# Half-row mask matmuls, casts with heads outermost and a new order of the first quarter in an attention and gated MLP kernel

## The chip, the cores and the metric

The kernel runs on one core of one Trainium2 chip. The metric is device time in microseconds, the median of several runs. A core has five engines that run side by side, each in its own order: TensorE (PE; its weight loads are shown as PEld), VectorE (DVE), ScalarE (ACT), GpSimd (POOL) and SyncE (SP, which here only issues DMAs). Profiles use the short names.

## The reference

Four sequences of 768 tokens with 8 heads of 64: causal attention, in which heads 0, 2 and 6 see everything before them and the other five see only the first 4 tokens and the last 64. Its output, 3072 rows of 512, goes through a two-layer MLP with the gate h / (1 + exp(-beta h)).

```python
scores = scale * np.matmul(q, k.transpose(0, 1, 3, 2))
rel = pos[:, None] - pos[None, :]
stream_keep = (rel >= 0) & ((pos[None, :] < 4) | (rel < 64))
scores = np.where(mask, scores, -1e9)      # mask: causal, or stream_keep
a = softmax(scores); x = a @ v             # then heads side by side: 3072 x 512
h = x @ w_in                               # 512 -> 2048
out = (h / (1 + np.exp(-beta * h))) @ w_out
```

## The kernel before

**Chunks and units.** The work is cut into 8 chunks (a half of a sequence, 384 rows, in three tiles of 128), taken in an order in which two sequences alternate. A chunk has 4 units of two heads each. Unit u belongs to chunk u // 4; units 0 to 7 (chunks 0 and 1) are the first halves of the first two sequences, so all their keys lie in their own 384 rows. The two heads of a unit lie in partitions 0 to 63 and 64 to 127 of KT and QT, so the two score matmuls of a pair use different row halves of TensorE.

**One unit** goes through: a load of q and k in float32 (SP, four heads at a time, into a tile s0 or s1 with the layout k/q, head, tile, 64), a cast to bf16 into qkb (L246), three transposes on TensorE each for k and q (L322), copies out of PSUM to KT (L330) and QT (L333), scores into a pair of PSUM banks sp in two steps (L451), exponentials on ACT into es (L460), the products with the values (L532), a division (L541, L545) that gives x, and for two units at a time the transposes of x (L570) and their copy to xT (L579). Streaming heads also need the sink tokens' keys and values beside the window's (KO, L312; VO, L259 and L260).

**Masks.** In chunks 0 and 1 a mask is added ahead of the scores: a matmul with the identity as weights (L422; "sp<-Ns,idb", "sp<-Nc,idb") writes 0 or -1e9 into the bank, and the scores are accumulated on top. Nc is causal, Ns has the three kinds of block of a streaming head. Unit 5 is an exception: its mask is multiplied after the exponential (L478, the word "ma"). From unit 8 on all masks are multiplied (Mh, Mc).

**MLP.** With xT of a chunk, G1 makes 16 groups of 128 features: four matmuls of 384 columns (L600), tanh on ACT (L605), and the gate on DVE (L608). G2 (L653) sums over the 16 and ends in a scaled copy (L657) and a store (L659). The weights come in four quarters each, by DMAs that POOL issues (L140 w_in, L144 w_out); a quarter of w_in holds four groups. The first 32 groups run as eight of chunk 0, eight of chunk 1, the other eight of chunk 0, the other eight of chunk 1.

**Order.** The order on every engine is the order in which the program emits instructions; there is no other scheduler. The first quarter is written out by hand in the string RAMP, one word per step, and the rest in PLAN. A word is a kind, a unit or chunk, for some a part, and an engine (v, a, g): ck and cq cast k or q, tk and tq transpose, kk and kq copy out of PSUM, ko copies sink keys, ad opens a pair of score banks and adds the mask, qk the scores, ex the exponentials, ma multiplies masks, pv a third of the value products, no divides, xx and cx transpose and copy x, cv and vo cast and copy values, lq and lv load, wi and wo issue a quarter of the weights, ro a piece of chunk 2's or a later chunk's rows, mm, mA and mb run a group of G1 (into mm or into an sp bank) or a step of G2, hm and hf the halves of one group, be the transposes of beta, ne, on and ml prepare masks and ones, and zz issues matmuls of zeros that keep TensorE busy.

**Buffers.** qkb has four buffers, so unit u's cast waits for the transposes of unit u - 4. PSUM has two pairs of banks sp for scores and three single banks mm for everything else of the ramp. QT has three buffers.

## Time and profile before

| | |
|---|---|
| median of 3 runs | 229.45 us (228.44, 229.45, 230.8) |
| profiled execution: span, first to last instruction | 227.0 us; 2.45 us below the median of the runs; its device time is not listed by itself |
| TensorE clock granted | 0.999 of full |
| PE, PEld busy | 219.4 us (97%), 126.4 us (56%) |
| DVE, ACT, POOL busy | 142.1 us (63%), 154.0 us (68%), 87.3 us (38%) |
| chain that ended last | PE 89%, DMA 4%, DVE 2%, SP's queue 2% |
| DMA | 31.66 MB, mean 139 GB/s |

Busy time of PE adds up what instructions take from start to end, and matmuls overlap in its pipeline, so the spacing of their starts tells what each really occupies. A line such as "14.50 0.51 PE L322 MATMUL mm<-idb,qkb 128*128 128x128 bf16 x6" in the order of time reads: start, length, engine, line, operation, output from inputs, size of the weights, the moving operand, and how many; what stands in brackets is idle time of that engine ahead of it and what ended it. The rows of a grouped view give busy time in us, the mean in ns, and idle time before.

### The profile page before, as it was taken

The numbers are of one execution on the slowest core, as the hardware profiler recorded it, in microseconds if no ns is written. First come the engines' busy times: TensorE is split into PE (matmuls) and PEld (weight loads), VectorE is DVE, ScalarE is ACT, GpSimd is POOL, SyncE is SP. The second block draws the span as 40 slices with busy tenths as digits, with TensorE's granted clock in tenths as the row PEclk, the third lists the DMA queues.
The fourth block names the chain that finished last, engine by engine and source line by source line (L and its number), as shares of the span: only waits on it lengthen the run. The fifth ranks groups of instructions, "written<-read, shape, count | busy, mean of one in ns | idle before, by whom it ended". The sixth has DMA issues, their size and how long they took to land.

```text
span 227.0 us, 5019 instructions
## 1 busy us (share of the span) xinstructions
PE 219.4 (97%) x1898; PEld 126.4 (56%) x1917; DVE 142.1 (63%) x342; ACT 154.0 (68%) x254; POOL 87.3 (38%) x143
## 2 busy tenths in 40 slices
...
GB/s 204 262 301 239 225 197 198 195 220 171 149 216 178 161 153 144 141 175 133 103 131 162 126 151 140 92 133 103 216 64 107 24 81 0 49 46 46 0 49 92
DMA packets 95383, 31.66 MB, mean 139 GB/s; under 512 B 81776, under 2 KB 92416, under 8 KB 95360
## 3 DMA queue, kind: packets, MB, share of 16 engines
...
q10 hardware_dynamic: 576, 0.40, 0.6%
...
## 4 chain that ended last, share of the span: by engine, by line
PE 89%; DMA 4%; DVE 2%; SPq 2%; issue 1%; ACT 0%; ACTq 0%; DVEq 0%
PE mm L653 34%; PE mm L600 25%; PE sp L600 12%; PE sp L451 6%; PE po L532 6%; DMA s<-in_k_dram 3%; DMA s<-in_q_dram 2%; PE mm L638 2%; DVE es L478 1%; PE mm L322 1%; SPq L132 1%; PE mm L570 1%; PE mm L451 1%; SPq L119 1%; PE sp L422 1%
## 5 line engine op out<-in xcount | busy, mean ns | idle before, releaser
L653 PE MATMUL mm<-w_out_sb,gT 128*128 128x512 bf16 x349 | 84.1, 379 | 1.3 <-issue 0.5
L460 ACT ACTIVATE es<-sp 128x768 bf16<-128x768 f32 (+2 forms) x72 | 56.5, 837 | 19.6 <-PE sp L451 19.4
L600 PE MATMUL mm<-xT,w_in_sb 128*128 128x384 bf16 x348 | 64.6, 326 | 0.0
L600 PEld LDWEIGHTS <-w_in_sb 128*128 128x128 bf16 x512 | 47.8, 98 | 29.7 <-issue 0.2
L605 ACT ACTIVATE th<-mm,beta_h 128x384 f32<-128x384 f32 x87 | 49.8, 588 | 5.6 <-PE mm L600 0.9
L653 PEld LDWEIGHTS <-gT 128*128 128x128 bf16 x368 | 33.4, 98 | 36.0 <-issue 1.5
L608 DVE SCALAR_TENSOR_TENSOR gT<-th,mm 128x384 bf16<-128x384 f32 x87 | 46.8, 551 | 7.4 <-ACT th L605 3.8
L282 POOL DMA_DIRECT2D s<-in_q_dram x30 | 22.4, 761 | 27.2 <-DMA QTD<-s 21.7
L600 PE MATMUL sp<-xT,w_in_sb 128*128 128x384 bf16 x164 | 32.3, 326 | 0.0
L657 ACT ACTIVATE osb<-mm 128x512 f32<-128x512 f32 x23 | 13.8, 602 | 26.1 <-PE mm L653 25.8
L532 PEld LDWEIGHTS <-es 128*128 128x128 bf16 x472 | 23.3, 98 | 13.6 <-issue 1.5
L608 DVE SCALAR_TENSOR_TENSOR gT<-th,sp 128x384 bf16<-128x384 f32 x41 | 22.3, 552 | 5.6 <-ACT th L605 3.7
L532 PE MATMUL po<-VX,es 128*128 128x65 bf16 x360 | 24.9, 194 | 0.8 <-ACT VX L251 0.4
L605 ACT ACTIVATE th<-sp,beta_h 128x384 f32<-128x384 f32 x41 | 23.8, 586 | 2.3 <-PE sp L600 0.2
L282 POOL DMA_DIRECT2D s<-in_k_dram x30 | 22.4, 759 | 6.8 <-DMA w_out_sb<-in_moe_w_out_dram 5.2
L251 POOL CAST VX<-vs 128x512 bf16<-128x512 f32 x16 | 10.6, 662 | 34.6 <-DMA vs<-in_v_dram 31.8
L541 DVE RECIPROCAL rec<-po 128x6 f32<-128x6 f32 x28 | 5.4, 193 | 27.0 <-PE po L532 27.0
L478 DVE TENSOR_TENSOR es<-es,Mh 128x768 bf16<-128x768 bf16 (+1 forms) x26 | 17.4, 698 | 5.0 <-ACT es L460 4.4
L451 PE MATMUL sp<-QTD,KT 64*128 64x128 bf16 (+2 forms) x258 | 19.2, 240 | 0.6 <-ACT QTD L333 0.3
L545 DVE TENSOR_TENSOR x<-po,rec 128x384 bf16<-128x384 f32 x28 | 15.6, 557 | 1.0
L451 PEld LDWEIGHTS <-KT 64*128 64x128 bf16 x278 | 11.1, 94 | 5.8 <-issue 3.6
L259 POOL COPY VO<-VX 128x512 bf16<-128x512 bf16 x16 | 10.0, 649 | 7.3 <-DVE VX L251 7.3
...
## 6 DMA issues: line engine op xcount, KB each, us to landing
...
```

Source lines behind the costliest of these rows:

```text
L251: copy(out=VX[b % 2][:, h2 * HT + t, :, 0:D], in_=staged["v", c][:, t])
L282: nc.gpsimd.dma_start(out=ROWS[c % 2, name][:, t, i * 4 * D:(i + 1) * 4 * D].rearrange("p (h d) -> p h d", d=D), in_=src[b, i:H:2, r:r + 1 ...
L451: nc.tensor.matmul(sps[i][r][:, x * 128:y * 128], key(a, lhs), s["QT"][half(a), qi * 128:(qi + y - x) * 128], start=first, stop=first or y ...
L460: nc.scalar.activation(out=views[i].rearrange("p r k j -> p r (k j)"), in_=banks[2][:, :, 0:n * 128], func=ACTF.Exp, scale=scale)
L478: nc.vector.tensor_mul(ev[:, :, 0:n], ev[:, :, 0:n], Mh[h2][:, None, m0:m0 + n].to_broadcast([128, 2, n, 128]))
L532: nc.tensor.matmul(po[:, qi, hh, :], e, val, start=(j == 0), stop=(j == len(lst) - 1))
L545: nc.vector.tensor_mul(xg[g][:, :, :, u % 2, :].rearrange("p a t d -> p t a d"), po[:, :, :, 0:D], rec.to_broadcast([128, HT, 2, D]))
L600: nc.tensor.matmul(hp[:, 0:HALF], w_in_sb[:, mo, fi * 128:(fi + 1) * 128], xT[c][:, mo, :], start=(mo == 0), stop=(mo == MO - 1))
L605: nc.scalar.activation(out=th, in_=hp[:, 0:HALF], func=ACTF.Tanh, scale=beta_h[:, fi:fi + 1])
L608: nc.vector.scalar_tensor_tensor(out=gTs[c][:, fi, :], in0=th, scalar=1.0, in1=hp[:, 0:HALF], op0=ALU.add, op1=ALU.mult)
L653: nc.tensor.matmul(op, gTs[c][:, fi, ns * 128:(ns + 1) * 128], w_out_sb[:, fi, :], start=(fi == 0), stop=(fi == FO - 1))
L657: nc.scalar.activation(out=osb, in_=op, func=ACTF.Copy, scale=0.5)
```

## The change

- **Masks of units 0 to 7.** Nq holds the kinds of block (causal, and three for streaming heads), made on POOL; folded() copies it into Nt, whose halves hold, for row half r and query half h, a block's weights for one head. An addition is now, per head and block, two matmuls with 64 rows of Nt as weights and 64 columns of the identity as moving operand (128 columns where one block serves two tiles). The two heads of a unit use the two row halves, in turns. Unit 5 is masked in this way too; "ma" is gone from the ramp. The masks Mh and Mc for later units are made later, on POOL (late_masks).
- **Casts.** qkb holds k first, and the cast walks heads outermost, so that it reads 192 consecutive numbers at a time. cast_both casts k and q of a unit in one instruction: units 0 (ACT), 1 and 3 (DVE) and 5 (POOL).
- **Order.** RAMP is new, with fillers as words (zi). PLAN is not touched. The matmuls of zeros read one block of 128 columns four times.

Two functions for two units at once (words wk, wq, yk, yq) and an engine for masks are added and not used by the new RAMP. The core of the diff:

```diff
...
         both = stage.tile([128, 2, 4, HT, D], F32, name=f"s{g}")
+        both_of[c, g] = both
...
+    zeros = consts.tile([128, 128], BF16, name="zeros")
+    nc.vector.memset(zeros, 0.0)
+    still = zeros[:, None, :].to_broadcast([128, 4, 128])
...
-    zeros = consts.tile([128, 512], BF16, name="zeros")
-    nc.vector.memset(zeros, 0.0)
...
     def idle(n, pool, name):
         for i in range(n):
             nothing = pool.tile([128, 512], F32, name=name)
-            nc.tensor.matmul(nothing, zeros[:, 0:128], zeros, start=True, stop=True)
-    idle(9, ps_m, "mm")
+            nc.tensor.matmul(nothing.rearrange("p (n j) -> p n j", n=4), zeros, still, start=True, stop=True)
...
-    own_masks, old_mask = Mh[0][:, 0:3:2], Mh[0][:, 1]
-    nc.vector.memset(Mh[0][:, 0:3], 1.0)
-    select(own_masks, 1, -1, window_i - 1, 2)
-    select(old_mask, 1, -1, -(128 - window_i + 1), 1)
-    nc.gpsimd.memset(Mh[0][0:n_sink_i, 0:2], 1.0)
-    select(own_masks, -1, 1, 0, 2)
-
-    Ns = consts.tile([128, 5 * 128], BF16, name="Ns")
-    Nc = consts.tile([128, 256], BF16, name="Nc")
     Mc = consts.tile([128, 128], BF16, name="Mc")
-    nc.gpsimd.memset(Nc, 0.0)
-    nc.gpsimd.affine_select(out=Nc.rearrange("p (r j) -> p r j", r=2), in_=Nc.rearrange("p (r j) -> p r j", r=2), compare_op=ALU.is_ge, fill=NEG, base=0, pattern=[[0, 2], [1, 128]], channel_multiplier=-1)
-
-    def negatives(which):
-        if 2 in which:
-            nc.vector.tensor_scalar(out=Mc, in0=Nc[:, 0:128], scalar1=0.0, scalar2=None, op0=ALU.is_ge)
-        a, n = which[0], len(which)
-        nc.vector.tensor_scalar(out=Ns[:, a * 128:(a + n) * 128], in0=Mh[0][:, a % 3 + a // 3:3].rearrange("p r j -> p (r j)"),
-                                scalar1=-1.0, scalar2=-NEG, op0=ALU.add, op1=ALU.mult)
+
+    def late_masks(part):
+        if part == 0:
+            nc.gpsimd.memset(Mh[0][:, 0:3], 1.0)
+            nc.gpsimd.memset(Mc, 1.0)
+        if part == 1:
+            select(Mh[0][:, 0:3:2], 1, -1, window_i - 1, 2)
+            select(Mh[0][:, 1], 1, -1, -(128 - window_i + 1), 1)
+            nc.gpsimd.memset(Mh[0][0:n_sink_i, 0:2], 1.0)
+        if part == 2:
+            select(Mh[0][:, 0:3:2], -1, 1, 0, 2)
+            select(Mc, -1, 1, 0, 1)
+
+
+    Nq = consts.tile([128, 4, 128], BF16, name="Nq")
+    Nt = consts.tile([128, 2, 4, 128], BF16, name="Nt")
+
+    def negative(buf, cm, step_, base, n):
+        nc.gpsimd.affine_select(out=buf, in_=buf, compare_op=ALU.is_ge, fill=NEG, base=base,
+                                pattern=[[0, n], [step_, 128]][2 - min(n, 2):], channel_multiplier=cm)
+    nc.gpsimd.memset(Nq, 0.0)
+    negative(Nq[:, 0], 1, -1, 0, 1)
+
+    def negatives(part):
+        if part == 0:
+            negative(Nq[:, 1:3], -1, 1, window_i - 1, 2)
+            negative(Nq[:, 3], -1, 1, -(128 - window_i + 1), 1)
+            nc.gpsimd.memset(Nq[:, 2:4, 0:n_sink_i], 0.0)
+            negative(Nq[:, 1:3], 1, -1, 0, 2)
+
+    def folded(some, copy):
+        for r in range(2):
+            for h in range(2):
+                copy(out=Nt[64 * r:64 * r + 64, h, some], in_=Nq[64 * h:64 * h + 64, some])
...
-        copy(out=s["qkb"][:, "qk".index(name)], in_=staged[name, c, p // 2][:, p % 2:4:2].rearrange("p h t d -> p t h d"))
+        copy(out=s["qkb"][:, "kq".index(name)].rearrange("p t h d -> p h t d"), in_=staged[name, c, p // 2][:, p % 2:4:2])
...
+    def cast_both(u, copy):
+        c, p = u // NPAIR, u % NPAIR
+        s = st_u.setdefault(u, {})
+        s["qkb"] = att.tile([128, 2, HT, 2, D], BF16, name="qkb", bufs=4)
+        copy(out=s["qkb"].rearrange("p i t h d -> p i h t d"), in_=both_of[c, p // 2][:, :, p % 2:4:2])
...
+            todo = []
             for r in range(2) if u < 8 and u not in on_vector else ():
                 n = len(dict.fromkeys((e[2], e[5]) for e in tiles[i][r] if added(e)))
                 m = tiles[i][r][0][5]
-                neg = Nc[:, 0:n * 128] if m is None else Ns[:, m * 128:(m + n) * 128]
-                nc.tensor.matmul(sps[i][r][:, 0:n * 128], ident, neg, start=True, stop=False)
+                kinds = [(0, 0, n)] if m is None else [((2, 3, 1, 3, 1)[m + x], x, 1) for x in range(n)]
+                todo.append([(r, h, *y) for y in kinds for h in range(2)])
                 covered[i, r] = n
+            opened_ = set()
+            while any(todo):
+                for some in todo:
+                    if some:
+                        r, h, kind, x, n = some.pop(0)
+                        rows_ = slice(64 * r, 64 * r + 64)
+                        nc.tensor.matmul(sps[i][r][:, x * 128:(x + n) * 128].rearrange("p (n j) -> p n j", n=n)[:, :, 64 * h:64 * h + 64], Nt[rows_, h, kind],
+                                         ident[rows_, None, 64 * r:64 * r + 64].to_broadcast([64, n, 64]), start=(r not in opened_), stop=False)
+                        opened_.add(r)
...
+            ends = {r: (r, x, y) for r, x, y, e in seq}
             for r, x, y, (a, lhs, qi, val, diag, m) in seq:
-                first = x >= covered.get((i, r), 0)
+                whole = (i, r) not in covered
                 nc.tensor.matmul(sps[i][r][:, x * 128:y * 128], key(a, lhs), s["QT"][half(a), qi * 128:(qi + y - x) * 128],
-                                 start=first, stop=first or y == covered[i, r])
+                                 start=whole, stop=whole or (r, x, y) == ends[r])
...
-        def mask(i):
+        def mask(i, eng=nc.vector):
             ev = views[i]
             ms = [[x for x, e in enumerate(tiles[i][r]) if e[5] is not None] for r in range(2)]
             if ms[0] and ms[0] == ms[1]:
                 n = len(ms[0])
                 m0 = tiles[i][0][0][5]
-                nc.vector.tensor_mul(ev[:, :, 0:n], ev[:, :, 0:n], Mh[h2][:, None, m0:m0 + n].to_broadcast([128, 2, n, 128]))
...
     def keep_busy(n):
 
         for i in range(n):
-            nc.tensor.matmul(sums_bank(0), zeros[:, 0:128], zeros, start=True, stop=True)
+            nc.tensor.matmul(sums_bank(0).rearrange("p (n j) -> p n j", n=4), zeros, still, start=True, stop=True)
...
+        elif what == "cb":
+            cast_both(n, copies[eng])
...
-            negatives([(0, 1, 2), (3, 4)][n])
+            negatives(n)
+        elif what == "fo":
+            folded([slice(0, 1), slice(1, 4)][n], copies[eng])
+        elif what == "mh":
+            late_masks(n)
...
-            late[n].pop(0)()
+            late[n].pop(0)(copies[eng or "v"])
         elif what == "tt":
             run(steps_T(n))
+        elif what == "zi":
+            idle(n, ps_m, "mm")
         elif what == "zz":
             keep_busy(n)
...
     RAMP = """
-        ck0g ne1 lv0.0 lv0.1 tk0 ck2a ne0 cq0v ck1a zz3 tq0 kq0a zz3 ad0.0 on0v lv0.2 kk0v cq1v tq1 qk0.0 tk2 ad0.1
-        kq1v tk1 kk1v lq1.0g be qk0.1 ex0.0 zz3 ad1.0 cv0.0g ko1 lq1.1 ex0.1 pv0 ck3v cq3g tk3 lv1.0g cq2a tq2 kk3v
-        lv1.1 cv0.1g ad1.1 qk1.1 kk2v ex1.1 tq3 ko2 qk1.0 wi0 vo0 cq4g lv1.2 cv0.2a lq2.0g ko3 pv0 kq2v pv0 ad2.0
-        qk2.0 lv2.0 ex1.0 pv1 kq3a pv1 ck4v ad2.1 qk2.1 lv2.1 pv1 ex2.0 ad3.0 tq4 no0 tk4 ex2.1 ck7g kk4a qk3.0 ad3.1
-        qk3.1 no1 pv2 ck6v ex3.0 cq5v ck5g pv2 tk6 xx0 ad4.0 cq6g pv3 kq4v ex3.1 pv2 ad4.1 cx0v ad5.0 qk4.1 pv3 lv2.2
-        no2 on1g tq5 pv3 qk4.0 kk6a ml0 tk5 cq7g kq5v ex4.1 kk5a ko5 ko6 ad5.1 tq6 wi1 qk5.0 ex4.0 tk7 tq7 ex5.0 no3
-        qk5.1 ex5.1 kq6v xx1 ad6.0 kk7v wi2 kq7v wi3 cx1a qk6.0 ml1 ad6.1 ex6.0 cv1.1g ko7 qk6.1 cv1.0v ex6.1 hm lq2.1
-        ma5.0 ma5.1 mm cv1.2g vo1 mm wo0 pv4 lv3.0g ad7.0 lv3.1 pv4 hf pv4 no4 qk7.0 ad7.1 pv5 pv5 ex7.0 lv3.2 qk7.1
-        pv5 no5 ml1 wo1 ex7.1 pv6 pv6 wo2 mm pv7 rq pv7 pv7 no7 wo3 pv6 no6 rk cq8g xx2 ro3 cx2a mA mA ck8g xx3 cx3a
-        mm mA mm mA mm mm mA mm mm mm mA mm ro3 mm mm mA mm mm mm ro3 mA mm ro3 mA mm ro3 mm mm ro3 mA mA mb mb tt8 mb
-        mb mb
+        zi8 lv0.0 cb0a ne0 fo1v zz3 cb1v tk0 tq0 on0v tq1 fo0g lv0.1 ck2v lv0.2 zz2 cb3v tk1 lq1.0 ad0.0 ad0.1 zz3
+        kk0a kq0a tk2 qk0.0 kk1a kq1v lq1.1 kk2v qk0.1 cq2g ex0.0 be zz3 ad1.1 ko1 zz1 cv0.1g tq2 tk3 ex0.1 wi0 ko2
+        lv1.0g cv0.0v kq2v ad1.0 cv0.2v lv1.1 lv1.2 qk1.0 qk1.1 kk3v ex1.0 ex1.1 tq3 ad2.0 ck4v kq3a qk2.0 lq2.0 pv0
+        lv2.0 vo0 pv0 pv1 ad2.1 ex2.0 pv0 pv1 qk2.1 lv2.1 ad3.0 pv1 no0 pv2 cq4g cb5g ko3 ex2.1 tq4 no1 qk3.0 ex3.0
+        tk4 kk4v kq4a tq5 ad3.1 qk3.1 xx0 ad4.1 ck6v qk4.1 kq5v cq6a cx0v pv2 tk6 ex3.1 ck7g pv2 mh0 no2 ad4.0 tk5
+        mh1 pv3 pv3 cq7g on1v kk6v qk4.0 mh2 mlg pv3 tq6 kk5v lv2.2 ex4.1 ko5 ko6 ad5.0 qk5.0 ex4.0 wi1 no3 tq7
+        lq2.1 kq6a ad5.1 ex5.0 qk5.1 wo0 xx1 wi2 tk7 cv1.1g cx1v ad6.1 ml1 ex5.1 cv1.0v kq7a qk6.1 ex6.1 ad6.0 kk7a
+        qk6.0 mm mm cv1.2v ko7 ex6.0 lv3.0 pv4 hm vo1 wi3 pv4 hf pv4 pv5 pv5 no4 ad7.1 qk7.1 ad7.0 qk7.0 pv5 no5 pv6
+        pv6 ex7.0 pv6 ex7.1 wo1 mm wo2 pv7 no6 pv7 xx2 pv7 cx2a ml1 no7 mA ck8g rq wo3 mA rk xx3 mm cx3v mA mm lv3.1
+        mm mm ro3 mA mm mA ro3 mm ro3 mA lv3.2 ro3 mm mA mm mA mm mA mm mm mA cq8g mm mA mm ro3 mm mm ro3 mA mA mb
+        mb tt8 mb mb mb
     """
     words = RAMP.split()
     on_vector = {int(w[2]) for w in words if w.startswith("ma")}
```

40 lines of the change are left out of this document (32 added, 8 removed).

## The prediction

> **What bounds the kernel now.** I read the windows first, then the chain that ended last, then each engine in order of time. The columns of a window are its length, TensorE's busy time (instructions), the granted clock, the DMA share and GB/s.
>
> ```profile
> core 0: 227.0 us, clock 0.999
> 4.96:22.00 17.04, 15.74 (x203) 1.00 1.20 272
> 22.00:46.04 24.04, 24.04 (x200) 1.00 1.21 204
> 46.04:227.00 180.96, 176.00 (x1494) 1.00 0.88 117
> ```
>
> From 22.00 to 46.04 us TensorE never rests, at full clock, and after that for under 5 us in 181. The first 22 us are different: there the chain runs through loads, and from about 17 us on it is TensorE's own work:
>
> ```profile
> 1.32 4.09 DMA s<-in_q_dram
> 9.35 5.93 DMA s<-in_k_dram
> 17.13 0.15 PE po L532 x5
> 17.28 0.22 PE sp L422 x2
> 18.00 0.17 PE mm L322 x3
> 23.86 0.32 PE sp L422 x2
> ```
>
> These rows (start, length, what, count) also give what a matmul really occupies, which the busy times of single instructions, being latencies, do not: 30 ns for 65 columns (0.15 / 5), 56 for 128 (0.17 / 3), 110 for 256 (0.22 / 2), 160 for 384 (0.32 / 2).
>
> The built order of the changed kernel differs from the old one on TensorE only in its first part: the last 3105 of its rows are the same, one for one, and SP's list of DMAs is the same throughout. So the time changes by what happens up to there. I compare up to the last mark that both ramps have, the second x transposes (xx3, at 28.80 us in a row below), behind which L600 runs densely. A microsecond before it is a microsecond at the end, as TensorE hardly rests afterwards.
>
> **Where the first part hangs.** On the loads of chunk 1:
>
> ```profile
> 13.94 0.50 POOL L246 CAST qkb<-s 128x384 bf16<-128x384 f32 x1 [0.22 <-DMA s<-in_q_dram]
> 14.50 0.51 PE L322 MATMUL mm<-idb,qkb 128*128 128x128 bf16 x6
> ```
>
> Unit 4's q lands, is cast by 14.44, and its transposes (tq4) start at 14.50. In the new order tq4 stands at the same place, behind the same cast on POOL and the same load. Ahead of it stand the same scores, masks and value products, and one third of pv2 more (two 65-column matmuls, 0.06 us). So the questions are whether the new order reaches tq4 late, and how long it needs from there.
>
> **Up to tq4: half a microsecond of cover.** Fillers and casts:
>
> ```profile
> 1.29 3.83 PE L167 MATMUL mm<-zeros 128*128 128x512 bf16 x9 [1.29 <-DVE zeros L157]
> 8.77 0.82 PE L513 MATMUL po<-zeros 128*128 128x512 bf16 x3
> 9.43 0.49 PE L422 MATMUL sp<-Ns,idb 128*128 128x384 bf16 x2
> 12.12 0.31 PE L532 MATMUL po<-VX,es 128*128 128x65 bf16 x5 [0.40 <-ACT VX L251]
> L251 DVE CAST VX<-vs 128x512 bf16<-128x512 f32 x5 | 2.1, 437 | 0.0
> L246 DVE CAST qkb<-s 128x384 bf16<-128x384 f32 x9 | 4.8, 543 | 1.5 <-DMA s<-in_k_dram 1.5
> L171 POOL TENSOR_SCALAR_AFFINE_SELECT Mh<-Mh 128x256 bf16<-128x256 bf16 x2 | 0.8, 408 | 0.8 <-DVE Mh L177 0.7
> L460 ACT ACTIVATE es<-sp 128x768 bf16<-128x768 f32 x15 | 11.8, 820 | 2.1 <-PE sp L451 2.1
> ```
>
> There is one cold filler (zi) less, 0.43 each (3.83 / 9), and the zeros come first on VectorE and are a quarter as wide, so they start some tenths earlier. Warm ones (zz) go from 9 to 12, at (9.43 - 8.77) / 3 = 0.22 each: +0.66 us, most of it where TensorE waits for casts or exponentials anyway; uncovered they would cost all of it.
>
> Casts on VectorE with heads outermost are not in the trace. Bounds for one of 384: 0.54 as the old one, and 384 / 512 x 0.437 = 0.33 by L251, whose runs are contiguous. The runs become 192 elements long, so I take a value near L251's, 0.37, and 0.57 for two tensors at once (0.66 to 1.08 by the same two rows is the slow side). [...]
>
> Making the new masks costs nothing: POOL's ten instructions for Nq and its share of Nt, at 0.41 or less from 1.4 on, end by 5.5, and ad0, the first to read them, comes near 6.9; past that 1.4 of cover they would cost one for one.
>
> Walked by these prices, the new order does this. Fillers end near 5.3; tq1 waits for unit 1's cast (load 1.32 + 4.09, cast 0.57) until 6.0; with zz2, tk1, ad0, zz3 and tk2 (0.44 + 0.17 + 0.17 + 0.66 + 0.17, four changes of rows at 0.10) unit 0's scores end near 8.4. Its two exponentials (0.8 each) end near 10; ad1.0 stands behind them and 0.9 of fillers. Unit 1's scores end near 10.7, its first exponential near 11.6, which gives ad2.0 its bank. qk2, pv0, pv1 and ad3.0 end by 13.9: 0.5 before tq4. The old order was no better off: it idled 0.4 and more before 12.12, and again before 14.50. What is lost or won ahead of tq4 is absorbed within that 0.5 and counts one for one beyond it. I put 0 (0 to +0.8).
>
> **From tq4 to the mark, 14.30 us before.** The masks:
>
> ```profile
> L422 PE MATMUL sp<-Ns,idb 128*128 128x384 bf16 x8 | 2.1, 324 | 0.0
> L422 PE MATMUL sp<-Ns,idb 128*128 128x256 bf16 x8 | 1.7, 276 | 0.0
> L422 PE MATMUL sp<-Nc,idb 128*128 128x256 bf16 x6 | 1.3, 272 | 0.0
> L422 PE MATMUL sp<-Nc,idb 128*128 128x128 bf16 x6 | 1.0, 219 | 0.0
> 17.11 0.38 PE L422 MATMUL sp<-Nc,idb 128*128 128x256 bf16 x2
> 17.43 0.34 PE L451 MATMUL sp<-QTD,KT 64*128 64x128 bf16 x6
> 17.70 0.30 PE L532 MATMUL mm<-VX,es 128*128 128x65 bf16 x4
> 21.61 1.64 DVE L478 TENSOR_TENSOR es<-es,Mh 128x768 bf16<-128x768 bf16 x2
> ```
>
> Before: 28 of them, 8 x 160 + 14 x 110 + 6 x 56 = 3.16 us, of which 1.54 behind tq4 (seven additions: 0.22, 0.11, 0.22, 0.22, 0.22, 0.33, 0.22). After: 124 half-row matmuls, 112 of 64 columns and 12 of 128. Unit 5 gets them too, since no "ma" word is left, and its two DVE products (1.64 us) go. Behind tq4 they make 34 narrow slots (28 pairs of two heads, 6 single ones) and 4 wide pairs. L451's six half-row matmuls of 128 take (17.70 - 17.43 - 0.10) = 0.17 us, so a wide pair costs 56 ns like one matmul. For a narrow pair the nearest row is L532's (65 columns, own weights each, 30 ns). Bounds: 27 (64 columns at the rate of 384) and 60 (the halves one after the other). I take 30: 34 x 30 + 4 x 56 = 1.24 us, so -0.30 (-0.40 to +0.55).
>
> Changing between full and half rows costs 0.10 each way: two 256-column matmuls from 17.11 end at 17.33, the half rows start at 17.43; their three pairs end at 17.60, the full rows start at 17.70. An addition next to its product saves a change now, one that stands alone pays two. Counted in both orders behind tq4: 20 before, 18 after, -0.20; over the whole ramp 32 in both.
>
> Stalls:
>
> ```profile
> 16.50 0.28 PE L422 MATMUL sp<-Nc,idb 128*128 128x128 bf16 x2
> 16.91 0.22 PE L532 MATMUL mm<-VX,es 128*128 128x65 bf16 x2
> 18.49 0.65 PE L322 MATMUL mm<-idb,qkb 128*128 128x128 bf16 x6
> 19.41 0.34 PE L451 MATMUL sp<-QTD,KT 64*128 64x256 bf16 x4 [0.26 <-ACT KT L330]
> ```
>
> Before: 16.61 to 16.91, and 19.41 - 18.49 less six transposes (0.34) and a change (0.10): 0.30 + 0.48, with small ones 0.9. In the new order ad4.0 waits for a score bank, and on ACT stand ex3.0, kq4a, cq6a and ex3.1 ahead (0.8 + 0.5 + 0.5 + 0.6, a copy or cast of 384 taken like L246's). qk3.0 ends near 14.8, so they end near 17.2, while TensorE comes to ad4.0 near 16.9: 0.3 to 0.5. tq6 waits for kk6v, which stands on DVE behind no2 and on1v: 0.3. tq5 and xx0 wait 0.3 together for cb5g and kk4v. Sum 1.0, so +0.10 (-0.9 to +0.9). The third of pv2 done earlier: -0.06.
>
> **The weights.**
>
> ```profile
> L140 POOL DMA_DIRECT2D w_in_sb<-in_moe_w_in_dram x1: 742/742/742, 19.9 to 19.9; - x1
> DMA to landing us min/median/max: 7.0/7.0/7.0
> L140 POOL DMA_DIRECT2D w_in_sb<-in_moe_w_in_dram x2: 750/756/762, 20.6 to 21.4; - x2
> DMA to landing us min/median/max: 10.1/11.4/12.7
> 27.50 1.46 PE L600 MATMUL sp<-xT,w_in_sb 128*128 128x384 bf16 x8
> 28.80 0.50 PE L570 MATMUL mm<-idb,x 128*128 128x128 bf16 x6
> L478 DVE TENSOR_TENSOR es<-es,Mh 128x768 bf16<-128x768 bf16 x3 | 1.6, 548 | 0.0
> L478 DVE TENSOR_TENSOR es<-es,Mh 128x512 bf16<-128x512 bf16 x1 | 1.2, 1179 | 0.0
> ```
>
> The second quarter of w_in lands at 26.9 (19.9 + 7.0). The fifth group of L600 needs it and starts at 27.50, only 0.6 later. The new order issues it on POOL behind the late masks (mh, ml), ko5 and ko6, by my walk 0.5 later, and TensorE comes to the group 0.45 earlier (the terms above), at 27.05. It lands between 26.9 (if the transfers ahead of it set its time) and 27.4: 0 to 0.4, I take +0.20. A quarter of w_out now goes ahead of the third and fourth of w_in. They move one place back: the third from 30.7 to 34.1, the fourth from 34.1 to some 37.5 by the same spacing. Ten and fourteen groups (0.65 each) behind the mark's transposes they are needed near 35.4 and 38.0: margins of 1.3 and 0.5.
>
> **Sum.** 0 - 0.30 - 0.20 + 0.10 - 0.06 + 0.20 = -0.26, so 226.7 us of span. The median of the three runs (228.44 to 230.8) is 229.45, 2.45 over the profiled span: **229.2 us**, no change. A measurement of this kernel can tell about 1% (2.3 us) from none.
>
> **Rivals.** (1) *The weights come late: slower.* For: the margins of 0.6 and 0.5 are the thinnest I found, and POOL has more to do ahead of wi1. DVE and POOL can hold each other up, too: the 512-column product took 1179 ns where those of 768 took 548. It decides once wi1 slips by more than 0.15, and from there a microsecond costs a microsecond. A slip of 1.5, three such hold-ups of 0.5, gives 1.15 over the forecast: 230.4. Against: POOL waits in places ahead of wi1, which cover part. [...]
> (2) *The stalls vanish: faster.* If the 1.0 behind tq4 stays away and the weights are in time: -1.2 more, 228.0. For: four casts fewer, 1.64 us off DVE. Against: ACT's queue ahead of ad4.0 is counted from rows.
> (3) *The halves don't overlap: the change doesn't do what it says.* 60 ns a pair: +0.84 behind tq4 and, beyond the 0.5 of cover, some 0.2 before; the weights are in time then (-0.20): 230.0. For: each half loads its own weights, 124 loads for 28. Against: L451's pairs.
>
> **Chances.** Forecast 0.58 (its own range 228.4 to 229.9), weights late 0.18, stalls vanish 0.14, halves serial 0.10. With the runs' scatter of 1.0% the range is 227.7 to 231.3. Faster by over 1% needs rival 2 and a further microsecond: 0.11. Slower by over 1% needs a slip of 2.6, or rivals 1 and 3 together: 0.13. Within: 0.76.
>
> **What would show it.** Right: tq4 near 14.5; Nt pairs 30 ns apart and 0.10 at each change of rows; the fifth group of L600 at 27.0 to 27.4, the mark near 28.5; clock 1.00. Wrong: tq4 after 15, a group of L600 that waits over 1 us for w_in, or TensorE idle behind 40 us where it was not.

## The result and the profile after

The changed kernel takes 229.93 us (median of 20 runs, 228.93 to 231.69), the kernel before 228.62 us in the same comparison: a ratio of 1.0046, with a 95% interval of 1.0025 to 1.0067. The medians lie 1.31 us apart; by the ratio the changed kernel is slower by about 1.05 us, against 0.25 us faster in the prediction: under the 1% that the prediction calls no change, but on the other side of zero.

The profiled execution is the fastest of the 20. In 144 executions of the kernel before, a run's time lay 1.86 us over its span (the median; 1.84 with the changed kernel). So the 227.0 us of the profile before stand for 228.86, and the 227.1 below for 228.93, a full microsecond under the changed kernel's median. One profile can't show where that microsecond goes, and so the experiments are read by their own traces, several of the same ramp. One disturbed execution of fill_gap (its profiled one, 323.91 us) and three of the kernel before (376 to 954 us) are left out everywhere, and the ratios, but not the medians, also leave out executions more than 1.5% above the fastest of their version.

First the windows, cut where the prediction cut them (first L654 group, first L707; G1 stands at L654, G2 at L707 now):

```profile
core 0: 227.1 us, clock 0.997
...
4.96:22.57 17.61, 14.98 (x283) 10.18 (x282) 12.46 (x32) 11.87 (x22) 11.61 (x27) 1.00 1.17 256
22.57:46.44 23.87, 23.78 (x213) 15.04 (x212) 20.28 (x43) 21.30 (x37) 11.04 (x18) 1.00 1.20 205
```

The columns are window, its length, busy time and instructions of PE, PEld, DVE, ACT and POOL, the granted clock, DMA share and GB/s. From the first MLP group on TensorE is as dense as before; ahead of it, it is busy for 15.0 of 17.6 us. The order of time shows where it rests:

```profile
14.50 0.34 PE L365 MATMUL mm<-idb,qkb 128*128 128x128 bf16 x3 [0.31 <-POOL qkb L264]
...
17.18 0.28 PE L586 MATMUL po<-VX,es 128*128 128x65 bf16 x4
18.69 0.23 PE L474 MATMUL sp<-idb,Nt 64*128 64x64 bf16 x4 [1.23 <-ACT es L514]
...
20.71 0.29 PE L474 MATMUL sp<-idb,Nt 64*128 64x64 bf16 x8
20.84 0.22 PE L505 MATMUL sp<-QTD,KO 64*128 64x128 bf16 x2
...
27.64 1.47 PE L654 MATMUL sp<-xT,w_in_sb 128*128 128x384 bf16 x8
28.94 0.50 PE L624 MATMUL mm<-idb,x 128*128 128x128 bf16 x6
```

tq4 starts at 14.50, as forecast. Unit 4's masks (ad4.0) start only at 18.69, behind a rest of 1.23 us. The fifth group of G1 comes at 27.64 and the mark at 28.94, 0.14 later than before and 0.4 later than forecast. The chain that ended last (start, length, what) names what the rest hangs on:

```profile
9.91 7.64 DMA s<-in_q_dram
...
17.64 0.51 ACT qkb L264
18.15 0.51 ACT es L514
...
18.69 0.23 PE sp L474 x4
18.93 0.29 PE mm L365 x3
...
19.24 0.57 DVE KT L373
...
19.86 0.53 POOL KO L355 x2
20.39 0.70 POOL w_in_sb L141
21.09 0.74 POOL w_out_sb L145
```

The last q load of chunk 1 is issued at 9.91 and lands at 17.56. ACT waits for it with cq6a (17.64), ex3.1 stands behind that in ACT's order, and ad4.0 waits for the bank that ex3.1 frees. From there it runs on, through unit 6's transposes, kk6v and KO, to the issue of w_in's second quarter on POOL, and in the end to that of the fourth, which lands at 38.58, just ahead of the group that needs it (38.63). The time from issue to landing of the last k and the last q load of chunk 1 (the shorter, the mean and the longer, which is the q's), first in the kernel before, then in the changed one:

```profile
DMA to landing us min/median/max: 5.9/6.3/6.6
```

```profile
DMA to landing us min/median/max: 5.7/6.7/7.6
```

The trace has 16 completions for that q, as many as there are DMA engines (I take them as one from each), and they say more than the row. Before, they come from 15.74 to 16.54 us. After, fifteen come from 15.81 to 16.20 and the sixteenth at 17.56.

### The profile page after: what moved, and what is told of

The parts are those of the page before. It is cut to its first block, busy times and chain, and to the rows that moved or that the text cites. A ratio compares the mean times of both kernels' runs of the same rounds, so it can differ in the third digit from the quotient of the medians.

```text
span 227.1 us, 5211 instructions
## 1 busy us (share of the span) xinstructions
PE 218.5 (96%) x1996; PEld 127.2 (56%) x2015; DVE 140.1 (62%) x342; ACT 153.5 (68%) x253; POOL 88.7 (39%) x144
## 4 chain that ended last, share of the span: by engine, by line
PE 81%; DMA 11%; POOL 2%; SPq 2%; issue 1%; ACT 1%; DVE 0%; ACTq 0%; POOLq 0%
PE mm L707 35%; PE mm L654 21%; PE sp L654 10%; DMA w_in_sb<-in_moe_w_in_dram 6%; PE po L586 6%; PE sp L505 6%; DMA s<-in_q_dram 5%; PE mm L692 2%; SPq L120 1%; SPq L133 1%; PE mm L505 1%; PE mm L365 1%; POOL w_in_sb L141 1%; PE mm L624 0%; POOL KO L355 0%
## 5 line engine op out<-in xcount | busy, mean ns | idle before, releaser
L707 PE MATMUL mm<-w_out_sb,gT 128*128 128x512 bf16 x349 | 84.0, 379 | 1.3 <-issue 0.5
L514 ACT ACTIVATE es<-sp 128x768 bf16<-128x768 f32 (+1 forms) x72 | 56.6, 836 | 20.7 <-PE sp L505 20.4
L654 PEld LDWEIGHTS <-w_in_sb 128*128 128x128 bf16 x512 | 47.6, 98 | 30.0 <-DMA w_in_sb<-in_moe_w_in_dram 0.5
L654 PE MATMUL mm<-xT,w_in_sb 128*128 128x384 bf16 x340 | 63.6, 326 | 0.1
L707 PEld LDWEIGHTS <-gT 128*128 128x128 bf16 x368 | 33.4, 98 | 36.0 <-issue 1.5
L659 ACT ACTIVATE th<-mm,beta_h 128x384 f32<-128x384 f32 x85 | 48.6, 588 | 5.6 <-PE mm L654 0.6
L662 DVE SCALAR_TENSOR_TENSOR gT<-th,mm 128x384 bf16<-128x384 f32 x85 | 45.7, 552 | 6.9 <-ACT th L659 3.4
L654 PE MATMUL sp<-xT,w_in_sb 128*128 128x384 bf16 x172 | 33.9, 326 | 0.0
L662 DVE SCALAR_TENSOR_TENSOR gT<-th,sp 128x384 bf16<-128x384 f32 x43 | 23.5, 552 | 5.8 <-ACT th L659 3.6
L659 ACT ACTIVATE th<-sp,beta_h 128x384 f32<-128x384 f32 x43 | 24.9, 585 | 2.5 <-PE sp L654 0.2
L269 POOL CAST VX<-vs 128x512 bf16<-128x512 f32 x14 | 9.0, 640 | 30.8 <-DMA vs<-in_v_dram 30.2
L532 DVE TENSOR_TENSOR es<-es,Mh 128x768 bf16<-128x768 bf16 (+1 forms) x24 | 14.3, 620 | 5.0 <-ACT es L514 4.4
```

The source lines that it names most:

```text
L514: nc.scalar.activation(out=views[i].rearrange("p r k j -> p r (k j)"), in_=banks[2][:, :, 0:n * 128], func=ACTF.Exp, scale=scale)
L532: eng.tensor_mul(ev[:, :, 0:n], ev[:, :, 0:n], Mh[h2][:, None, m0:m0 + n].to_broadcast([128, 2, n, 128]))
L654: nc.tensor.matmul(hp[:, 0:HALF], w_in_sb[:, mo, fi * 128:(fi + 1) * 128], xT[c][:, mo, :], start=(mo == 0), stop=(mo == MO - 1))
L659: nc.scalar.activation(out=th, in_=hp[:, 0:HALF], func=ACTF.Tanh, scale=beta_h[:, fi:fi + 1])
L662: nc.vector.scalar_tensor_tensor(out=gTs[c][:, fi, :], in0=th, scalar=1.0, in1=hp[:, 0:HALF], op0=ALU.add, op1=ALU.mult)
L707: nc.tensor.matmul(op, gTs[c][:, fi, ns * 128:(ns + 1) * 128], w_out_sb[:, fi, :], start=(fi == 0), stop=(fi == FO - 1))
```

## The experiments

There were 18 runs in five groups, each group on one chip with the kernel before beside it. The last two columns are from the one profiled execution: where the last of chunk 1's q landed, and where w_in's second quarter did. "Low clock" counts executions with a mean granted clock under 0.995; the kernel before had none among 144.

| run | median us | ratio to before [95%] | low clock | q | w_in 2nd |
|---|---|---|---|---|---|
| changed kernel | 229.93 | 1.0046 [1.0025, 1.0067] | 5 of 20 | 17.56 | 27.44 |
| again | 229.89 | 1.0064 [1.0032, 1.0097] | 4 of 12 | 17.44 | 27.38 |
| order_w | 229.37 | 1.0042 [1.0012, 1.0072] | 3 of 12 | 18.01 | 28.49 |
| v_first | 229.79 | 1.0055 [1.0030, 1.0080] | 2 of 12 | 17.36 | 27.25 |
| both | 229.39 | 1.0033 [1.0010, 1.0057] | 2 of 12 | 17.42 | 27.36 |
| fill_gap | 229.91 | 1.0061 [1.0039, 1.0083] | 0 of 6 | | |
| ex_first | 229.97 | 1.0060 [1.0043, 1.0078] | 0 of 5 | 17.26 | 29.17 |
| order_ex | 229.99 | 1.0040 [1.0012, 1.0069] | 0 of 12 | 17.88 | 26.50 |
| wi_late | 229.76 | 1.0022 [0.9990, 1.0053] | 0 of 12 | 17.67 | 29.30 |
| again2 | 229.42 | 1.0033 [1.0014, 1.0052] | 1 of 12 | 17.34 | 27.29 |
| wi1_early | 229.07 | 1.0039 [1.0012, 1.0065] | 3 of 12 | 17.98 | 26.31 |
| order_wi1 | 230.11 | 1.0060 [1.0026, 1.0093] | 4 of 9 | 18.27 | 25.98 |
| order_wi1_ex | 229.29 | 1.0018 [0.9985, 1.0050] | 2 of 12 | 17.40 | 25.48 |
| full_0to3 | 229.28 | 1.0025 [1.0002, 1.0049] | 0 of 12 | 16.59 | 28.21 |
| full_all | 229.98 | 1.0058 [1.0032, 1.0084] | 1 of 9 | 16.24 | 29.14 |
| before_quarters | 228.88 | 1.0020 [0.9994, 1.0046] | 0 of 12 | 18.01 | 27.85 |
| best_try | 228.22 | 0.9994 [0.9974, 1.0014] | 0 of 12 | 16.34 | 25.91 |
| before_wo0 | 228.47 | 0.9999 [0.9987, 1.0011] | 0 of 12 | 16.53 | 27.22 |

fill_gap2 (fill_gap once more): 229.50, 1.0045 [1.0018, 1.0072], 0 of 12, 18.00, 27.30.

### First group: the order of the weights, and what stands ahead of them on POOL

again is the changed kernel.

> The changed kernel itself, as the measure for the others. Its profiled execution on record was the fastest of its 20 runs (228.93 us; median 229.93), and in it the fourth quarter of w_in landed at 38.58 us with the group that needs it starting at 38.63. Theory W (weights late): a second profile, nearer to the median, shows a TensorE wait of 0.5 to 1.2 us for a quarter of w_in between 27 and 40 us, and a first L707 row after 46.5 us. Theory Q (the last chunk-1 q lands late and holds ACT, and so the mask words of unit 4, up): the wait near 17.2 us is again 1.0 to 1.4 us, and it is all. If neither: the extra time lies behind 46 us. Ratio to the kernel before 1.002 to 1.007.

order_w:

```diff
-        ... qk5.1 wo0 xx1 wi2 tk7 ... hm vo1 wi3 pv4 ...
+        ... qk5.1 wi2 xx1 wi3 tk7 ... hm vo1 wo0 pv4 ...
```

> The changed kernel with the quarters of the weights issued in the old order: the second, third and fourth of w_in, then the first of w_out. Theory W: the fourth quarter of w_in lands near 35.3 us instead of 38.6, no group waits for it, and the median falls by 0.6 to 1.2 us, ratio to the kernel before 0.999 to 1.002. Theory Q: the wait near 17.2 us stays at 1.2 us and the ratio stays at 1.0045.

v_first:

```diff
-        ... ex0.1 wi0 ko2 lv1.0g cv0.0v ...
+        ... ex0.1 lv1.0g ko2 wi0 cv0.0v ...
```

> The changed kernel with the memset that opens the buffer of v for chunk 1, and KO of unit 2, ahead of the first quarter of w_in on POOL. Theory Q: w_in's first quarter is issued near 11.5 us instead of 10.9, the last q of chunk 1 lands near 16.6 us instead of 17.56, the wait ahead of unit 4's mask words falls from 1.2 to 0.2 to 0.5 us, and the second x transposes come near 28.1 instead of 28.94. If the weights don't bind (theory W wrong) the median falls by 0.7 to 1.0 us, ratio 1.000 to 1.002; if they do, the groups behind only wait for w_in instead, and the ratio stays at 1.003 to 1.005.

both has the two edits.

> Both edits: the old order of the weight quarters, and the memset of v's buffer ahead of the first of them. Theory W and Q together: 1.5 to 2.0 us less than the changed kernel, ratio to the kernel before 0.995 to 0.998, no TensorE wait over 0.5 us between 17 and 46 us. W alone: as with the old order alone, 0.999 to 1.002. If the new masks cost time in themselves (rival H: the halves one after the other), it stays at 1.002 or more.

None of it brought the kernel before back. With the old order the fourth quarter of w_in landed at 35.55 instead of 38.3 to 38.6, as expected, and the median was 0.5 lower, within the scatter. The quarter issued at 11.30 instead of 10.92 left the q near where it was (17.36). In again's trace the rest ahead of unit 4's masks was 0.9 us, and no group waited for w_in by more than 0.1. So both theories, in the sizes expected, are out. What again's trace bears out is the third reading in its text: the mark comes at 28.82 (28.80 in the kernel before) and the first L707 at 46.17 (46.04), but the span is 0.6 us longer, so most of that is lost behind 46 us. The part on why the prediction was wrong comes back to it. And the profiled execution of order_w, 1.2 us longer than the one on record, shows something that no forecast had. Its windows, with the granted clock third from the right:

```profile
14.50:17.60 3.10, 2.98 (x55) 2.10 (x56) 2.62 (x6) 1.46 (x3) 3.04 (x9) 1.00 1.19 242
17.60:19.15 1.55, 0.04 (x3) 0.06 (x2) 1.50 (x6) 1.06 (x3) 1.15 (x5) 1.00 1.22 230
19.15:20.90 1.75, 1.75 (x40) 1.21 (x39) 1.11 (x4) 1.39 (x3) 0.96 (x5) 0.97 1.31 248
20.90:24.20 3.30, 3.30 (x50) 2.44 (x48) 1.70 (x5) 2.55 (x6) 2.76 (x4) 0.50 0.90 200
24.20:28.00 3.80, 3.80 (x74) 2.76 (x73) 2.42 (x6) 3.40 (x7) 2.96 (x6) 1.00 1.17 231
```

TensorE rests for 1.5 us in the second row, the same rest ahead of ad4.0. It works again for 1.75 us, at a mean clock of 0.97, and then runs at 0.50 for 3.3 us. From unit 4's masks to the first group of G1 it takes 5.11 us (19.15 to 24.26) against 3.88 in the profile on record (18.69 to 22.57): 1.2 us lost, behind a rest that is over.

### Second group: the rest, ACT's order, and the first quarter of w_in

fill_gap: five products of zeros, in a bank of their own, in the rest.

```diff
-        ... pv2 mh0 no2 ad4.0 tk5 ...
+        ... pv2 mh0 no2 zy5 ad4.0 tk5 ...
+        elif what == "zy":
+            spot = ps_m.tile([128, 512], F32, name="mm")
+            for _ in range(n):
+                nc.tensor.matmul(spot.rearrange("p (n j) -> p n j", n=4), zeros, still, start=True, stop=True)
```

> The changed kernel with five 512-column products of zeros (0.22 us each at full clock) placed where TensorE waits 1.2 us ahead of unit 4's mask words (ad4.0), and nothing else; the wait itself stays. Theory G (the long rest makes the clock gate halve TensorE's clock for some 3.3 us a little later, in about one run of four: the profile of order_w shows 0.50 from 20.9 to 24.1 us behind a rest of 1.51 us): no run with a mean clock under 0.995, the mean falls by 0.3 to 0.5 us, and the slowest runs (231 us and over) are gone; the median of the undisturbed runs stays at 229.5. Rival: the lower clock comes from something else (the load, the chip): still 2 to 4 of 12 runs under 0.995.

ex_first:

```diff
-        ... ad3.1 qk3.1 xx0 ad4.1 ck6v qk4.1 kq5v cq6a cx0v pv2 tk6 ex3.1 ck7g ...
+        ... ad3.1 qk3.1 ex3.1 xx0 ad4.1 ck6v qk4.1 kq5v cq6a cx0v pv2 tk6 ck7g ...
```

> The changed kernel with ex3.1 (an exponential of unit 3) ahead of cq6a (the cast of unit 6's q, which waits for the last q load of chunk 1) on ACT. Theory Q in its ACT form: ex3.1 ends near 17.5 us instead of 18.7, unit 4's masks start near 17.6, the rest of 1.2 us shrinks to 0.2 to 0.4, a rest of up to 0.6 us appears ahead of unit 6's q transposes (tq6), the second x transposes come near 28.3; the clock stays at 1.00 in all runs; the weights still bind, so the median falls by only 0.3 to 0.8 us, ratio 1.001 to 1.004. If the load itself is the bound whatever stands behind it: the rest moves to tq6 in full and nothing is won.

order_ex is both and ex_first together.

> The old order of the weight quarters, v's memset ahead of the first of them, and ex3.1 ahead of cq6a. If weights, ACT's queue and the clock gate are the three causes: no lower clock, no wait for w_in, second x transposes near 28.2, median 228.0 to 228.6, ratio to the kernel before 0.997 to 1.001. If a further cause of about 0.8 us stays (the runs with both edits at full clock had a median of 229.2): 228.9 to 229.3.

wi_late:

```diff
-        ... ex0.1 wi0 ko2 lv1.0g cv0.0v ... ck7g pv2 mh0 no2 ad4.0 ...
+        ... ex0.1 lv1.0g ko2 mh0 wi0 cv0.0v ... ck7g pv2 no2 ad4.0 ...
```

> The changed kernel with v's memset, KO of unit 2 and the memsets of the late masks (mh0) ahead of the first quarter of w_in on POOL, so that the quarter is issued near 11.9 us (10.92 in the changed kernel, 11.30 in v_first, 11.55 in the kernel before). Theory L (w_in's first quarter, issued earlier, takes engine time from the last q of chunk 1): that q lands at 16.4 to 16.9 us instead of 17.4 to 17.6, and the rest ahead of unit 4's masks falls to 0.3 or less. If the q lands at 17.3 or later all the same, the quarter isn't what holds it up.

fill_gap had no low clock in its 6 runs, nor had ex_first in 5 and order_ex in 12; wi_late had none either, though its rest was 1.1 us long. So on this chip the rest made no difference to the clock, and fill_gap alone says nothing for theory G. Of the clock gate in that theory the traces show the granted clock alone (0.50 in order_w's); what sets it isn't shown. ex_first moved the rest as it should, in part: 0.6 us ahead of unit 6's q transposes, none over 0.5 ahead of ad4.0. Its median didn't fall, and order_ex missed its first forecast (228.0 to 228.6) by about a microsecond, with runs from 228.52 to 232.19. In wi_late the first quarter was issued at 11.90, later than before (11.55), and the q landed at 17.67 all the same: that quarter isn't what holds the q up. Its trace has a further loss, at the fifth group of G1 (what the transfer's tile shows: issue, who waited for it, time to landing; then the group in order of time):

```profile
L141 POOL DMA_DIRECT2D w_in_sb<-in_moe_w_in_dram x1: 757/757/757, 20.4 to 20.4; - x1
...
  PE sp L654: 1.4, 1
...
DMA to landing us min/median/max: 8.8/8.8/8.8
```

```profile
29.34 1.48 PE L654 MATMUL sp<-xT,w_in_sb 128*128 128x384 bf16 x8 [1.42 <-DMA w_in_sb<-in_moe_w_in_dram]
```

The second quarter of w_in took 8.8 us instead of 7.0 or 7.1, and TensorE waited 1.42 us for it. The prediction's first rival went by the margin of 0.6 us there; here it is used up.

### Third group: the second quarter earlier

again2 is the changed kernel once more; its text comes first. wi1_early:

```diff
-        ... lv2.2 ex4.1 ko5 ko6 ad5.0 qk5.0 ex4.0 wi1 no3 ...
+        ... lv2.2 ex4.1 wi1 ko5 ko6 ad5.0 qk5.0 ex4.0 no3 ...
```

> The changed kernel once more, on this chip, as the measure for the three others and for two counts. Theory V (the second quarter of w_in lands at 27.3 us in good runs and later in many, and the group that needs it at 27.4 to 27.6 waits): median 229.5 to 230.1, ratio 1.004 to 1.006, runs spread over 2 us. Theory G (clock gate): 2 to 4 of 12 runs with a mean clock under 0.995; if none, the lower clock depends on the chip.

> The changed kernel with the second quarter of w_in issued on POOL ahead of KO of units 5 and 6, near 19.1 us instead of 20.3, and nothing else. Theory V: the quarter lands near 26.0 to 26.5, the fifth group of L654 doesn't wait for it, the median falls by 0.3 to 0.8 us, ratio 1.001 to 1.003, and the later quarters (one place back still) hold the rest. Rival: its landing is set by the loads of chunks 1 and 2 on SP's queue, not by its issue: it lands at 27 or later as before, and nothing is won.

order_wi1 adds order_w to it, order_wi1_ex adds ex_first as well.

> The second quarter of w_in early, and the old order of the others. Theory V with W: all four quarters in time, median 228.6 to 229.0, ratio 1.000 to 1.002; what stays over the kernel before is the rest of 1.2 us ahead of unit 4's masks against what the masks and rows save.

> The same, and ex3.1 ahead of cq6a on ACT. All three causes out: second x transposes at 28.0 to 28.6 us, no wait for w_in, clock 1.00 in every run, median 227.8 to 228.6, ratio 0.996 to 0.999. If it is still over 1.002, the loss sits in the new casts or masks themselves.

again2 came in just under what was expected of it, at 229.42 and with one low clock. The quarter was issued at 19.5, 19.7 and 18.9 us in the three others and landed at 26.31, 25.98 and 25.48, and no group waited for it. In the twelve other profiles of the changed ramp with the quarter where it was, it landed at 27.2 to 29.3 in eleven, and TensorE waited 0.3 to 1.4 us for it in four. That part of theory V holds; the gain of 0.35 in the median (229.07 against 229.42) is within the scatter, and the ratio (1.0039) missed the 1.001 to 1.003 expected. order_wi1 missed: its q landed at 18.27, the rest was 1.9 us, and 4 of 9 runs had a low clock. order_wi1_ex has the shortest span of all profiles, with its mark at 28.25:

```profile
core 0: 225.9 us, clock 0.998
19.23 0.33 PE L365 MATMUL mm<-idb,qkb 128*128 128x128 bf16 x3 [0.60 <-DVE KT L373]
```

Its fastest run is 227.72, but the median, at 229.29, is over the forecast. What was still open was the q, late in every one of these.

### Fourth group: how many instructions TensorE has

DMA queue 8 carries instructions, in packets of 16 KB (16 of them, 0.26 MB, in the profile after). The windows of one microsecond with the first such packet (packets, MB, share of the 16 engines in that microsecond), the changed kernel from 14 to 15 us and the kernel before from 16 to 17:

```profile
q1 hardware_dynamic: 428, 0.32, 107.7%
q8 instruction: 1, 0.02, 7.1%
```

```profile
q1 hardware_dynamic: 349, 0.09, 51.8%
q8 instruction: 1, 0.02, 6.8%
```

7.1% of 16 engines for a microsecond is one engine for 1.1 us. The packet starts at 14.57 us after and at 16.76 before, when TensorE has started about as many matmuls and weight loads (307 and 281): the extra mask matmuls (96 in all), each with its weight load, bring it forward, into the time in which chunk 1's last q is on its way. One engine's part of that q is then late by about the length of the packet. The trace doesn't name the engine of a packet, so that the two meet on one engine is inferred from the times.

full_0to3 adds the masks of units 0 to 3 by full rows, full_all those of all eight (FULL is range(4) or range(8)); Nq, as it stands, serves as the weights:

```diff
+                if u in FULL:
+                    for j, (kind, x, w) in enumerate(kinds):
+                        nc.tensor.matmul(sps[i][r][:, x * 128:(x + w) * 128].rearrange("p (n j) -> p n j", n=w), Nq[:, kind],
+                                         ident[:, None, :].to_broadcast([128, w, 128]), start=(j == 0), stop=False)
+                    continue
```

> The changed kernel with the masks of units 0 to 3 added by full-row matmuls again (31 fewer matmuls and 31 fewer weight loads on TensorE); units 4 to 7 keep the halves. Theory I (instruction loads): TensorE's instructions come in loads of 16 KB, each some 1.1 us on one of the 16 DMA engines; the more instructions, the earlier the load. In the changed kernel it starts at 14.1 to 15.1 us and holds up the sixteenth part of chunk 1's last q (17.3 to 17.6, the other fifteen parts by 16.2); before it started at 16.8, behind that q (16.5). With 62 rows less the load comes at 16.3 to 17.2 and the q lands whole by 16.6; the rest ahead of unit 4's masks falls from 1.2 to 0.4 us or less, the first G1 group comes 0.5 to 1.0 earlier, the median falls by 0.3 to 0.9. Rival: the instruction load has nothing to do with it: the q stays at 17.3 or later.

> The changed kernel with all eight units' masks by full rows (the half-row masks undone, the rest of the change kept). Theory I: q by 16.6 as with units 0 to 3, and the masks behind 14.5 us cost 0.3 to 0.6 more on TensorE than the halves: median 0 to 0.6 under the changed kernel's, ratio 1.001 to 1.004. If the halves were the loss in themselves: ratio 0.999 or less.

before_quarters is the kernel before with more, smaller fillers:

```diff
-            nc.tensor.matmul(sums_bank(0), zeros[:, 0:128], zeros, start=True, stop=True)
+            for y in range(0, 512, 128):
+                nc.tensor.matmul(sums_bank(0)[:, y:y + 128], zeros[:, 0:128], zeros[:, 0:128], start=True, stop=True)
```

> The kernel before with each of its nine 512-column warm fillers (L513) cut into four of 128 columns: the same 0.22 us of TensorE each, but 27 more matmuls and 27 more weight loads. Theory I: the first instruction load starts at 13.5 to 15 us instead of 16.76, and the last q of chunk 1 (or the k, q ahead of it) lands 0.8 to 1.3 us later than 16.54, in one of its 16 parts; the second load comes ahead of 26.15 by some us. Its price: up to 1.0 us where the chain hangs on that q, ratio 1.000 to 1.004. Rival: nothing but the fillers' shape changes: q at 16.5, ratio 0.998 to 1.001.

best_try is full_0to3 and order_wi1_ex together.

> All edits that paid: full rows for units 0 to 3, ex3.1 ahead of cq6a, the second quarter of w_in ahead of KO of units 5 and 6, the old order of the other quarters. Theories I, W, V, G together: q by 16.6, no wait for w_in, no rest over 0.6 us, clock 1.00 throughout, and so runs less spread: median 227.4 to 228.3, ratio 0.994 to 0.998. If the spread stays (runs of 229.5 and more in a third of cases), something else than these four varies from run to run.

The q answers from both sides. With fewer instructions the packet starts at 15.38 (full_0to3), 15.85 (full_all) and 16.22 (best_try), and the q is whole at 16.59, 16.24 and 16.34. With 27 more matmuls of the same total time, the kernel before gets its packet at 15.28 instead of 16.76: fifteen parts of the q land by 16.64, the last at 18.01. The packet of full_0to3 came earlier than the 16.3 that I expected and cost that q 0.4 us instead of 1.3; where it starts alone doesn't settle what it holds up. But over all profiles the two go together: in the 13 whose first packet starts by 15.28 us one part of this q lands 1.0 to 2.0 us behind the other fifteen, and in the six where it starts at 15.38 or later 0.4 us behind at most. ex_first is one of these six: its packet starts at 16.09, and its q is late (17.26) only because it was issued late (10.87). before_quarters lost 0.4 us in the median, with an interval that takes in none. full_all missed its forecast (1.0058 against 1.001 to 1.004). From tq4 to the first group of G1 it takes 7.99 us against 7.26 in full_0to3, 0.15 of it by a longer rest, so the full rows of units 4 to 7 cost some 0.6 us there, as expected; and in its profile the second quarter of w_in was late again (29.14, a wait of 1.0 us).

best_try is the only version whose median (228.22) is under that of the kernel before in its group (228.49); its interval holds 1, though the ratio missed the 0.994 to 0.998 expected. The changed kernel's, 1.0025 to 1.0067, lies wholly above it. In its trace unit 4's masks follow at once, and what is left stands at unit 6's transposes:

```profile
17.32 0.28 PE L593 MATMUL po<-VX,es 128*128 128x65 bf16 x4
17.54 0.23 PE L481 MATMUL sp<-idb,Nt 64*128 64x64 bf16 x4
...
19.33 0.33 PE L365 MATMUL mm<-idb,qkb 128*128 128x128 bf16 x3 [0.59 <-DVE KT L373]
...
21.98 1.47 PE L661 MATMUL mm<-xT,w_in_sb 128*128 128x384 bf16 x8
```

### Fifth group: the weights alone, and the filled rest once more

before_wo0, in the kernel before:

```diff
-        ... kk7v wi2 kq7v wi3 cx1a ... vo1 mm wo0 pv4 ...
+        ... kk7v wo0 kq7v wi2 cx1a ... vo1 mm wi3 pv4 ...
```

> The kernel before with the first quarter of w_out issued ahead of the third and fourth of w_in, as in the changed kernel, and nothing else. Theory W: the third and fourth quarter of w_in land one place later, near 34.1 and 37.5 us instead of 30.75 and 34.09, at margins of 1.2 and 0.5 us: no wait in a good run, up to 0.5 us in others, ratio 0.999 to 1.002. If this placement were the whole loss of the changed kernel: 1.004 or more.

> The changed kernel with five products of zeros in the rest ahead of unit 4's masks, once more, since its first profile was disturbed. Theory G: TensorE rests for under 0.6 us there, the mean clock is over 0.995 in every run (the changed kernel with the rest left as it is: 10 of 44 runs under it), the mean is 0.2 to 0.4 us lower, the median the same within 0.3. Rival (the lower clock has another cause): 2 or 3 of 12 runs under 0.995.

In the kernel before w_out's first quarter ahead of the others costs nothing (0.9999). Its place by itself isn't the loss. fill_gap2 again had no low clock in 12 runs, so 0 of 18 with the rest filled against 10 of 44 in the changed kernel; but the two were never run on the same chip. Its median (229.50) and its ratio (1.0045) are those of the changed kernel, and two of its runs took over 231 us at full clock, so most of the loss stands without a lower clock. Its trace shows the fillers in place of the rest:

```profile
17.40 0.28 PE L586 MATMUL po<-VX,es 128*128 128x65 bf16 x4
17.52 1.24 PE L831 MATMUL mm<-zeros 128*128 128x512 bf16 x5
19.14 0.23 PE L474 MATMUL sp<-idb,Nt 64*128 64x64 bf16 x4 [0.37 <-ACT es L514]
```

Over all runs, 24 of 113 had a low clock where a rest of 0.8 us or more stood ahead of ad4.0 in the profile, and 3 of 80 where it was filled or shorter. By groups these counts don't single out the rest: 11 of 48 in the first group and 10 of 45 in the third (2 of 12 there without the rest, 8 of 33 with it), but 0 of 35 in the second, wi_late's rest of 1.1 us included.

## Why the prediction was wrong

**What held.** The chain through chunk 1's loads and tq4, which starts at 14.50. The masks: in the rows from 20.71 four pairs of 64 columns take 0.13 us, 32 ns each against 30. The changes of rows cost 0.10. The halves do overlap, so rival 3 is out. Of the new casts on VectorE, the one of two tensors: 0.56, and 0.57 was taken. The cast of one tensor did not hold: 0.47, 0.42 and 0.72, on average 0.54 as before, and 0.37 was taken:

```profile
5.38 0.56 DVE L324 CAST qkb<-s 128x768 bf16<-128x768 f32 x1 [0.56 <-DMA s<-in_q_dram]
6.02 0.47 DVE L264 CAST qkb<-s 128x384 bf16<-128x384 f32 x1
12.71 0.42 DVE L264 CAST qkb<-s 128x384 bf16<-128x384 f32 x1
15.90 0.72 DVE L264 CAST qkb<-s 128x384 bf16<-128x384 f32 x1
```

No row of the kernel before shows the 0.57, and twice the bounds of its two rows is 0.66 to 1.08; the run shows 0.56 for 768, half the time per element of the old casts (0.53 to 0.55 for 384). The casts of one tensor don't come out so in the ramp; behind it two take 0.35 and one 0.55 (at 49.01, 59.09 and 53.99 us), and why isn't shown.

**The step that failed: the stalls behind tq4, "Sum 1.0, so +0.10".** Of the 14.44 us from tq4 to the mark, TensorE rested 1.56 beyond the changes of rows (1.30, 0.16 and 0.10, by the spacing of the starts), and before 0.92 (0.30 and 0.48 as in the prediction, and 0.14 between the x transposes from 20.34 and the masks at 20.82): +0.64 instead of +0.10. The masks, the rows and the third of pv2 came to -0.50 in place of -0.56 (28.94 - 14.50 less 14.30, less 0.64), and the +0.20 for the weights to nothing, since the second quarter landed at 27.44 and its group started at 27.64. What I had "near 17.2", the end of ex3.1, was 18.66. The queue on ACT was counted rightly, by its durations; what stands at its head, cq6a, I had start when ACT came to it. Its input lands at 17.56 instead of 16.54, and I took the landing times of the loads as unchanged because SP's list of DMAs is the same. They weren't: instructions come by the same 16 DMA engines (the q8 row, 0.5% of the engines' span), and I counted the 96 added matmuls as time on TensorE alone. From the first packet to the second TensorE starts 160 to 250 matmuls and weight loads (its other instructions aren't in that count). Over the whole span 15 packets of 16 KB stand against 3815 matmuls and weight loads before, and 16 against 4011 after: 254 and 251 to a packet. That the packets are TensorE's is inferred from these counts. The list of DMA queues had its row for them before the change, too.

**A second step that failed: "So the time changes by what happens up to there."** The rows behind the mark are the same, but the time behind it is not. In the three profiles of the changed kernel the mark comes at 28.94, 28.82 and 28.72 us, 28.80 before, so next to nothing is lost ahead of it on average (0.26 was to be won); and yet two of the three spans are 0.6 us longer (227.6 against 227.0). The list of DMAs shows a sixteenth instruction packet and, among the last stores, one that lands late (KB each, median us to landing), first in the kernel before, then in the changed one:

```profile
q8 instruction: 15, 0.25, 0.5%
out_dram<-osb SPq DMA_DIRECT2D x1, 128.0 KB, 1.7
```

```profile
q8 instruction: 16, 0.26, 0.5%
out_dram<-osb SPq DMA_DIRECT2D x1, 128.0 KB, 3.1
```

The sixteenth packet starts at 223.26, into the third store from the end, of which fifteen parts land by 223.96 and the last at 225.38. All 13 profiles with 16 packets have this one late part; in none of the six with 15 packets is there one. From the start of G2's last matmul to the end of the span it is 3.73, 4.29 and 4.07 us in the changed kernel's three profiles, 3.79 on average in the 13, and 3.48 to 3.52 in the six. So some 0.3 us of the loss stands at the very end; no version was run that moves this packet alone.

**The clock.** "Clock 1.00" failed in 5 of 20 runs. In the changed kernel's 44 executions the ten with a low clock took 231.30 us on average, the others 229.58: 0.4 us of the mean. The new ramp brings it on: in the first and the third group 21 of 93 executions of it had a low clock, and none of 66 of the kernel before on the same chips. That it is the rest ahead of ad4.0 is argued from order_w's one profile and not shown, as the filled rest and the open one were run on different chips; the 3 of 80 that are left came in order_wi1_ex and full_all, with rests of 0.6 and 0.7 us ahead of unit 6's transposes. In order_w's profile a rest of 1.5 us came ahead of the 3.3 us at 0.50, and in order_wi1's one of 1.9 us was followed by no such stretch (mean clock 0.997, against 0.993 in order_w's), so the length of a rest alone doesn't tell what comes behind it.

**The weights.** The hold-up of DVE and POOL that the first rival names shows in the profile before: with no cast or copy of POOL beside them, DVE's products of 512 columns take 0.42 to 0.43 us (five of them), with one 1.18 and 1.68; and on POOL a copy of 512 to VO takes 0.61 to 0.67, but 0.94 beside one of DVE's slow products. The old casts on DVE keep their 0.54 to 0.55 beside POOL's. What the hold-up costs the weights no run shows. The direction of that rival was right, and its price is real in some executions: the second quarter of w_in lands at 27.3 in most profiles (27.4 in the sum), but at 28.2 to 29.3 in five of them, each worth 0.3 to 1.4 us of waiting where the group came in time. Its issue hangs on the same chain behind the late q. The third and the fourth quarter came 1.1 to 1.2 us later than in the prediction (35.26 and 38.58 against 34.1 and 37.5), which used up the margin of 0.5: the fourth's group starts just as it lands. TensorE waited 0.2 us for it at most in the profile on record, 0.4 in again2.

**The sum against the runs.** The 2.45 us between span and time was wrong too: a median of runs set against one span of another run. It is 1.86. By it the forecast's 226.7 would have been 228.6, and the loss to explain is the same.

**What stays open.** The mean of the runs at full clock is still 0.85 us above the kernel before (229.58 against 228.73). best_try, where the late q, ACT's order behind it, the place of w_in's quarters and, by its 15 packets, the last stores are put right at once, is level. No single one of them moved a median clear of the scatter, so apart from the 0.3 us at the end how the 0.85 splits is not shown. Why the second quarter takes 7 us in one execution and 9 in the next isn't shown either, and the new casts were not undone by themselves. And best_try undoes the halves in units 0 to 3, so the version that keeps all of the change (order_wi1_ex, 1.0018 [0.9985, 1.0050]) has not been shown to be level.
